# Seven products instead of eight in half of the first matmul, another seven-product form in the second, and the second attention visit moved into the second matmul

## The chip, the cores and the metric

The kernel runs on one core of one Trainium2 chip. TensorE (PE in the profile) multiplies matrices out of SBUF into PSUM, VectorE (DVE) and ScalarE (ACT) read PSUM and do the elementwise work, GpSimd (POOL) scales the values and issues the loads, SyncE (SP) issues the stores and the transposing DMAs. The metric is the device time of one execution in microseconds (us), lower is better.

## The reference

Inputs are q, k, v of shape (batch 4, heads 8, sequence 768, head dimension 64), one decay per head, and two weight matrices, 512 x 2048 and 2048 x 512. A causal linear attention with decay is followed by a feed-forward block with exact GELU:

```
for each block of 64 positions:
    out   = ((q k^T) * Dmask) v  +  (q * lam^(pos+1)) state
    state = lam^64 * state + (k * lam^(63-pos))^T v
x = out, 3072 tokens x 512
y = gelu(x @ w_in) @ w_out
```

## The kernel before

The 3072 tokens are cut into 24 chunks of 128 positions; a group is four chunks, one of each batch entry, 512 tokens. There are six groups (`NG = 6`), and for each the two matmuls run as a list of blocks that `mlp_blocks(g)` returns. Attention for the groups to come is put between these blocks as "visits": short runs of small TensorE products on quarters of the array. A visit answers one pair of chunks (`answer_states`, `answer_values`), asks the next (`ask`: scores into the two `sc` banks) and makes the products of keys and values for the states (`ask_products`). The order is written by hand: `at(when, run)` gives each step a place in the sequence of blocks, measured in the work of the blocks, and the final loop issues each block after the steps that are due. Every engine executes what it is given in that order.

PSUM has eight banks of 128 x 512 f32, handed out by tag: two each of `sc`, `mh` and `mo`, one each of `o` and `t`. SBUF tiles rotate in the same way through their `bufs`.

For groups 1 to 5 before the change:

- First matmul (`mm1`, line 518): 16 blocks of 128 rows of w_in against 512 tokens. Eight of them (in group 1: twelve) run in pairs on halves of 256 tokens, low half first, since the high half of `x_t` arrives by the group's first visit; the rest run on 512 columns. Each result, one bank, goes through one GELU on ScalarE (line 521) into `g_t`.
- Second matmul (`blocks_by_seven`, products on line 414): 2 x 2 x 2 quarters of the product, by seven products of 16 matmuls each instead of eight. Five sums of quarters of `g_t` (`g_sum`, line 389) and five of w_out (`w_out_sum`, line 368, once) are made on VectorE, and the seven results are combined by two ScalarE copies and seven VectorE additions. Each product is emitted in two steps `u` = 0, 1 of eight matmuls (128 tokens each). In the last group the products `m1` and `m7` of the two `u` are held in two different banks (`banks["r"]`).
- Visits: the first of a group stands one block into it, the second eight or ten blocks into it, inside the first matmul. Group 1, which ends the attention start-up, has visits at 0, 4, 14 and 20 blocks.

Of the kernel before, what the change touches and what calls it, by code (L numbers as in the profile page):

```python
# [10 lines left out]
ALU = mybir.AluOpType  # L11
# [4 lines left out]
def kernel(  # L16
# [34 lines left out]
    g_pool = ctx.enter_context(tc.tile_pool(name="g", bufs=2))  # L51
# [37 lines left out]
    w_out_t = w_pool.tile([128, NK2, d_model], BF16)  # L89
    NS = 4  # L90
# [66 lines left out]
    def decay_v(c, eng):  # L157

        c.v_dec = work_pool.tile([128, H, D], BF16, tag="vd", name="v_dec", bufs=4)
        eng.tensor_mul(c.v_dec, c.v, lam_m[:, :, None].to_broadcast((128, H, D)))  # L160
# [180 lines left out]
    def empty_outputs(c):  # L341
# [6 lines left out]
        else:  # L348
# [9 lines left out]
    W_SUMS = {1: (B11, B22, ALU.add), 3: (B12, B22, ALU.subtract), 4: (B21, B11, ALU.subtract),  # L358
              6: (B11, B12, ALU.add), 7: (B21, B22, ALU.add)}

    def w_out_sum(i, half):

        if i not in wsum:
            wsum[i] = w_pool.tile([128, KH, DH], BF16, name=f"w_sum{i}")
        (ka, da), (kb, db), op = W_SUMS[i]
        n = KH // 2
        at = lambda ks: slice(ks.start + half * n, ks.start + (half + 1) * n)
        nc.vector.tensor_tensor(wsum[i][:, half * n:(half + 1) * n, :], w_out_t[:, at(ka), da], w_out_t[:, at(kb), db],
                                op=op)

    def w_out_sums():
        for i, half in [(6, 0), (6, 1), (7, 0), (1, 0), (3, 0), (4, 0), (7, 1), (1, 1), (3, 1), (4, 1)]:
            w_out_sum(i, half)

    def blocks_by_seven(g, g_t, first):
# [5 lines left out]
        G_SUMS = {6: (0, hi, 0, lo, ALU.subtract), 1: (0, lo, KH, hi, ALU.add), 2: (0, hi, KH, hi, ALU.add),  # L381
                  5: (0, lo, KH, lo, ALU.add), 7: (KH, lo, KH, hi, ALU.subtract)}

        def g_sum(i, k):
            if i not in gsum:
                gsum[i] = sum_pool.tile([128, KH, TH], BF16, tag=f"g{i}", name=f"g_sum{i}")
            ka, ta, kb, tb, op = G_SUMS[i]
            ks = slice(k, k + n4)
            nc.vector.tensor_tensor(gsum[i][:, ks, :], g_t[:, ka + k:ka + k + n4, ta], g_t[:, kb + k:kb + k + n4, tb],  # L389
                                    op=op)  # L390
# [3 lines left out]
        def with_sums(i, run):  # L394
            def both():
                run()
                if i in sums_at:
                    g_sum((5, 2, 1, 6, 7)[sums_at.index(i)], 0)
            return both

        sums_at = range(10, 15)
        blocks = [(with_sums(i, run), cost) for i, (run, cost) in enumerate(first)]

        left = {1: lambda k, t: gsum[1][:, k, t], 2: lambda k, t: gsum[2][:, k, t],
                3: lambda k, t: g_t[:, k, t], 4: lambda k, t: g_t[:, KH + k, TH + t.start:TH + t.stop],
                5: lambda k, t: gsum[5][:, k, t], 6: lambda k, t: gsum[6][:, k, t], 7: lambda k, t: gsum[7][:, k, t]}
        right = {2: lambda k: w_out_t[:, k, d_lo], 5: lambda k: w_out_t[:, KH + k, d_hi]}
        right.update({i: (lambda k, i=i: wsum[i][:, k, :]) for i in W_SUMS})
# [3 lines left out]
        def product(i, u, o, begin):  # L412
            for k in range(KH):
                nc.tensor.matmul(o, left[i](k, slice(u * C, (u + 1) * C)), right[i](k),  # L414
                                 start=(begin and k == 0), stop=(k == KH - 1), skip_group_check=True)

        def tile_f(name):
            sb[name] = sum_pool.tile([128, 2, DH], F32, tag=f"f_{name}", name=f"f_{name}")
            return sb[name]

        def store(rows, us, cols):
            b = slice(rows * 2 + us.start, rows * 2 + us.stop)
            dst = out_r[g, :, b, cols]
            nc.sync.dma_start(dst, sb["o0" if rows == 0 else "o1"][:, us, cols])
# [3 lines left out]
        def m3(u):  # L428
            if u == 0:
                banks["p"] = bank([128, 2, DH], F32, "mo", "p_ps")  # L430
            product(3, u, banks["p"][:, u, :], u == 0)
            if u == 1:
                nc.scalar.copy(tile_f("e"), banks["p"])
                g_sum(5, n4)

        def m4(u):
            if u == 0:
                banks["q"] = bank([128, 2, DH], F32, "mo", "q_ps")
            product(4, u, banks["q"][:, u, :], u == 0)
            if u == 0:  # L440
                g_sum(2, n4)
            else:
                nc.scalar.copy(tile_f("f"), banks["q"])

        def m5(u):
            if u == 0:
                banks["p5"] = bank([128, 2, DH], F32, "mo", "p5_ps")
                g_sum(1, n4)
            product(5, u, banks["p5"][:, u, :], u == 0)
            if u == 1:  # L450
                sb["o0"] = out_pool.tile([128, 2, d_model], F32, tag="o0", name="o0_sb", bufs=1)
                nc.vector.tensor_add(sb["o0"][:, :, d_hi], sb["e"], banks["p5"])  # L452
                nc.vector.tensor_sub(tile_f("x1"), sb["f"], banks["p5"])
                if last:
                    store(0, both, d_hi)

        def m2(u):
            if u == 0:
                banks["q2"] = bank([128, 2, DH], F32, "mo", "q2_ps")
            product(2, u, banks["q2"][:, u, :], u == 0)  # L460
            if u == 0:
                g_sum(6, n4)
            else:
                sb["o1"] = out_pool.tile([128, 2, d_model], F32, tag="o1", name="o1_sb", bufs=1)
                nc.vector.tensor_add(sb["o1"][:, :, d_lo], sb["f"], banks["q2"])
                nc.vector.tensor_sub(tile_f("x2"), sb["e"], banks["q2"])

        def m1(u):
            if u == 0:
                banks["s"] = bank([128, 2, DH], F32, "mh", "s_ps")  # L470
                if last:
                    banks["r"] = [bank([128, DH], F32, tag, "r_ps") for tag in ("mh", "t")]
                else:
                    r_ps = bank([128, 2, DH], F32, "mh", "r_ps")
                    banks["r"] = [r_ps[:, 0, :], r_ps[:, 1, :]]
                    banks["r_all"] = r_ps
            product(1, u, banks["r"][u], u == 0 or last)
            if u == 0:
                g_sum(7, n4)
            elif last:  # L480
                for w in range(2):
                    nc.vector.tensor_add(sb["x2"][:, w, :], sb["x2"][:, w, :], banks["r"][w])
            else:
                nc.vector.tensor_add(sb["x2"], sb["x2"], banks["r_all"])

        def m6(u):
            product(6, u, banks["s"][:, u, :], u == 0)
            if u == 1:
                nc.vector.tensor_add(sb["o1"][:, :, d_hi], sb["x2"], banks["s"])
                store(1, both, every)  # L490

        def m7(u):
            product(7, u, banks["r"][u], False)
            if last:
                nc.vector.tensor_add(sb["o0"][:, u, d_lo], sb["x1"][:, u, :], banks["r"][u])
# [370 lines left out]
```

## Time and profile before

| | |
|---|---|
| median of three runs | 202.98 us (200.58 to 205.71) |
| the profiled execution's own time | 201.34 us |
| span in the profile | 199.6 us, granted TensorE clock 0.999 |
| TensorE busy | 191.0 us, 96% of the span |
| VectorE busy | 120.4 us, 60% |
| ScalarE busy | 82.7 us, 41% |
| GpSimd busy | 110.5 us, 55% |
| group 0 and start-up | 0 to 50.4 us |
| groups 1, 2, 3, 4, 5 begin at | 50.4, 81.1, 110.3, 139.9, 168.9 us |

The page names one execution. A group's duration is read from the start of its first w_in product to that of the next. A row of matmuls in the timeline gives a start, the duration to the modelled end of the last one, and the count; the distance between starts of rows gives the pace.

### The profile page before, as it was taken

Reading aid. Unit: us, or ns where it says so; the run is one execution under the profiler, and the core shown is the slowest. Engines: PE = TensorE matmul, PEld = TensorE weight load, DVE = VectorE, ACT = ScalarE, POOL = GpSimd, SP = SyncE. Lnnn points to the kernel's source line nnn. Section 1 sums busy time; section 2 is a strip of 40 time slices with the busy share of each in tenths; the row PEclk is TensorE's granted clock in tenths of the full one; section 3 lists DMA queues with packets and bytes.
Section 4 is the critical chain, followed back from the end, with each engine's and each line's share of the span. In section 5 each row is a group of like instructions: output and inputs, shape, how many; then the busy total and the mean of one; then the engine's idle time right before and its main releaser. Section 6 shows DMA issues by size and latency. Waiting matters only on the chain.

```text
span 199.6 us, 5998 instructions
## 1 busy us (share of the span) xinstructions
PE 191.0 (96%) x2625; PEld 142.9 (72%) x2636; DVE 120.4 (60%) x206; ACT 82.7 (41%) x149; POOL 110.5 (55%) x136
## 2 busy tenths in 40 slices
PE   7699999999999999999999989999999999999992
PEld 2388674455887788885688875688884788865881
DVE  3753507764473869694949658649638358341482
ACT  4964564234556413174520255520355410566200
POOL 8999973499969799993493497591400000000000
PEclk9999999999999999999999999999999999999999
DMA  5999999999999999999799799899700002300014
GB/s 115 148 174 175 200 204 206 153 216 150 130 220 149 151 142 136 118 209 233 72 84 153 234 68 127 90 110 122 234 8 3 3 0 80 134 0 3 0 53 158
DMA packets 102761, 24.76 MB, mean 124 GB/s; under 512 B 93264, under 2 KB 99920, under 8 KB 102736
## 3 DMA queue, kind: packets, MB, share of 16 engines
q0 software_dynamic: 81072, 13.38, 99.3%
q1 hardware_dynamic: 21664, 11.02, 26.6%
q8 instruction: 20, 0.33, 0.7%
q14 instruction: 5, 0.04, 0.1%
HBM read 27.27 MB, written 6.29 MB: 168 GB/s over the span
## 4 chain that ended last, share of the span: by engine, by line
PE 73%; DMA 10%; POOL 10%; DVE 4%; issue 1%; POOLq 0%; DVEq 0%
PE h_ps L518 35%; PE r_ps L414 8%; PE p_ps L414 8%; PE q_ps L414 8%; DMA q_t<-in_q_dram 6%; DMA w_out_t<-in_moe_w_out_dram 4%; PE s_ps L414 4%; POOL w_in_t L94 3%; PE o_ps L531 3%; POOL k_t L70 2%; POOL q_t L70 2%; POOL v_t L70 2%; PE o_ps L314 2%; POOL v_dec L160 1%; PE kv_ps L290 1%
## 5 line engine op out<-in xcount | busy, mean ns | idle before, releaser
L518 PE MATMUL h_ps<-x_t,w_in_t 128*128 128x256 bf16 (+3 forms) x648 | 87.5, 290 | 1.0 <-issue 0.6
L521 ACT ACTIVATE g_t<-h_ps 128x512 bf16<-128x512 f32 (+2 forms) x99 | 57.8, 584 | 72.6 <-PE h_ps L518 72.6
L518 PEld LDWEIGHTS <-w_in_t 128*128 128x128 bf16 x656 | 58.4, 98 | 23.8 <-issue 1.0
L389 DVE TENSOR_TENSOR g_sum<-g_t 128x1024 bf16<-128x1024 bf16 x50 | 33.4, 713 | 16.4 <-ACT g_t L521 16.4
L414 PEld LDWEIGHTS <-g_sum 128*128 128x128 bf16 x400 | 39.1, 98 | 4.8 <-issue 0.3
L160 POOL TENSOR_TENSOR v_dec<-v_t,lam_m 128x512 bf16<-128x512 bf16 x23 | 24.3, 1094 | 25.6 <-PE o_ps L326 14.8
L70 POOL DMA_DIRECT2D v_t<-in_v_dram x24 | 22.2, 927 | 3.1 <-DMA w_out_t<-in_moe_w_out_dram 1.7
L414 PE MATMUL r_ps<-w_sum,g_sum 128*128 128x256 bf16 x160 | 19.1, 273 | 0.1
L73 POOL DMA_DIRECT2D k_t<-in_k_dram x24 | 18.7, 799 | 0.0
L73 POOL DMA_DIRECT2D q_t<-in_q_dram x24 | 18.3, 788 | 0.0
L414 PEld LDWEIGHTS <-g_t 128*128 128x128 bf16 x160 | 15.6, 98 | 2.9
L531 PE MATMUL o_ps<-w_out_t,g_t 128*128 128x512 bf16 x61 | 14.5, 379 | 0.4 <-issue 0.3
L333 DVE TENSOR_TENSOR x_t<-o_ps,lam_q 128x512 bf16<-128x512 f32 x16 | 10.6, 683 | 3.9 <-PE o_ps L314 3.9
L70 POOL DMA_DIRECT2D k_t<-in_k_dram x12 | 11.2, 933 | 1.9 <-DMA w_out_t<-in_moe_w_out_dram 1.6
L70 POOL DMA_DIRECT2D q_t<-in_q_dram x12 | 10.9, 908 | 2.4 <-DMA w_out_t<-in_moe_w_out_dram 2.4
L531 PEld LDWEIGHTS <-g_t 128*128 128x128 bf16 x64 | 5.9, 98 | 6.3
L305 DVE TENSOR_TENSOR sc_m<-sc_ps,cmask_d 128x512 bf16<-128x512 f32 x16 | 10.3, 679 | 0.0
L452 DVE TENSOR_TENSOR o_sb<-f_e,p_ps 128x512 f32<-128x512 f32 x5 | 3.4, 686 | 11.0 <-issue 11.0
L582 PE MATMUL idle_ps<-idle 128*128 128x256 bf16 (+1 forms) x40 | 8.7, 353 | 1.2 <-DVE idle L107 1.2
L414 PE MATMUL p_ps<-w_out_t,g_sum 128*128 128x256 bf16 x80 | 9.6, 273 | 0.0
L414 PE MATMUL s_ps<-w_sum,g_sum 128*128 128x256 bf16 x80 | 9.6, 273 | 0.0
L414 PE MATMUL q_ps<-w_out_t,g_sum 128*128 128x256 bf16 x80 | 9.6, 273 | 0.0
(90 smaller groups left out, 192.2 us busy)
## 6 DMA issues: line engine op xcount, KB each, us to landing
out_dram<-o_sb SPq DMA_DIRECT2D x9, 512.0 KB, 4.9
v_t<-in_v_dram POOLq DMA_DIRECT2D x24, 128.0 KB, 5.6
w_out_t<-in_moe_w_out_dram POOLq DMA_DIRECT2D x4, 512.0 KB, 10.3
w_in_t<-in_moe_w_in_dram POOLq DMA_DIRECT2D x7, 256.0 KB, 7.3
k_t<-in_k_dram POOLq DMA_DIRECT2D x12, 128.0 KB, 6.5
q_t<-in_q_dram POOLq DMA_DIRECT2D x12, 128.0 KB, 6.8
k_t<-in_k_dram POOLq DMA_DIRECT2D x24, 64.0 KB, 4.8
q_t<-in_q_dram POOLq DMA_DIRECT2D x24, 64.0 KB, 5.0
```

Of the source, the lines that this page charges most:

```text
L70: nc.gpsimd.dma_start(raw[n, name], chunk_of(name, n))
L73: nc.gpsimd.dma_start(raw[n, name][:, r::2, :], chunk_of(name, n)[:, r * HP:(r + 1) * HP, :])
L94: nc.gpsimd.dma_start(w_in_t[:, :, f], w_in_r[:, :, f])
L160: eng.tensor_mul(c.v_dec, c.v, lam_m[:, :, None].to_broadcast((128, H, D)))
L305: nc.vector.tensor_mul(w.sc_m[:, hi], w.sc_ps[hi], cmask_d[:, None, None, :].to_broadcast((128, 2, HP, D)))
L333: nc.vector.tensor_mul(x[:, :, :, HALVES[t]], pairs[n].o_ps[t], lam_q[:, :, None, HALVES[t]].to_broadcast((128, HP, 2, D)))
L389: nc.vector.tensor_tensor(gsum[i][:, ks, :], g_t[:, ka + k:ka + k + n4, ta], g_t[:, kb + k:kb + k + n4, tb], op=op)
L414: nc.tensor.matmul(o, left[i](k, slice(u * C, (u + 1) * C)), right[i](k), start=(begin and k == 0), stop=(k == KH - 1), skip_group_check=True)
L518: nc.tensor.matmul(h_ps[:, k, :], w_in_t[:, ki, (kf + k) * 128:(kf + k + 1) * 128], x_t[:, ki, cols], start=(k == 0 and ki == 0), stop=(ki ...
L521: nc.scalar.activation(g_t[:, kf:kf + ks, cols], h_ps, ACT.Gelu)
L531: nc.tensor.matmul(om[io], g_t[:, kf, io * C:(io + 1) * C], w_out_t[:, kf, :], start=(kf == 0), stop=(kf == NK2 - 1))
L582: nc.tensor.matmul(idle_ps[0][:, :cols], idle[:, :128], idle[:, :cols], start=True, stop=True)
```

## The change

1. The second half of the first matmul of groups 1 to 5 (row blocks 4 to 7 and 12 to 15) is done by seven products too. `w_in_sums` makes four sums of w_in once; `x_sums` makes four sums of quarters of `x_t` in each group. Two `Step`s of seven products of four matmuls each work in three PSUM banks (`ha`, `hb`, `hc`): a product is written to a bank, copied to SBUF by ScalarE (`kept`), and the next product is accumulated onto the same bank. VectorE adds (`total`), and GELU reads three of the four results from SBUF. The other half of the first matmul stays plain, in pairs on 256 tokens, with the high-half blocks in the banks `t` and `o`.
2. The second matmul's seven products take a form with four sums of `g_t` and four of w_out. Three of its results are again accumulated onto a bank that has been read. The last two products, `m7` and `m4`, are read in two steps: after each `u` of `m7` VectorE adds that half of the bank, after each `u` of `m4` ScalarE copies it.
3. `g_t` becomes one tile, not two in rotation; `v_dec` has six buffers, not four.
4. The second visits stand 20 or 22 blocks into the group (21 in group 1), inside the second matmul, and the steps around them move: masks, sums of states, emptied outputs, GpSimd's `decay_v`. In group 1 the key-value products of the visit at 4 blocks take the `sc` banks.
5. In group 1 the products 7 and 4 of the second matmul are issued in halves of 128 columns.

The diff, cut to its core:

```diff
-    W_SUMS = {1: (B11, B22, ALU.add), 3: (B12, B22, ALU.subtract), 4: (B21, B11, ALU.subtract),
-              6: (B11, B12, ALU.add), 7: (B21, B22, ALU.add)}
+    W_SUMS = {1: (B12, B11), 2: (B22, 1), 3: (B22, B12), 4: (B21, 2)}
...
+    def first_blocks(g, g_t, x_t, mm1):
...
+        def x_sums():
+            for i in (1, 2, 3, 4):
+                x_s[i] = sum_pool.tile([128, 2, TH], BF16, tag=f"x{i}", name=f"x_sum{i}")
...
+                nc.vector.tensor_sub(x_s[i], a, b)
...
+            def product(self, i, b, tag=None):
+                if tag:
+                    self.banks[b] = bank([128, 2, TH], F32, tag, f"{b}_ps")
+                for k in range(2):
+                    for q in range(2):
+                        nc.tensor.matmul(self.banks[b][:, k, :], left[i](q, self.kf + k), right[i](q),
+                                         start=(tag is not None and k == 0 and q == 0), stop=(q == 1),
+                                         skip_group_check=True)
...
+            def kept(self, name, b):
+                self.sb[name] = sum_pool.tile([128, 2, TH], F32, tag=f"f_{name}", name=f"h_{name}", bufs=2)
+                nc.scalar.copy(self.sb[name], self.banks[b])
+            def total(self, name, b):
+                nc.vector.tensor_add(self.sb[name], self.sb[name], self.banks[b])
...
+            def p1(self):
+                self.product(1, "ha", "mh")
+                self.kept("p1", "ha")
+            def p2(self):
+                self.product(2, "hb", "mo")
+                self.total("p1", "hb")
+            def p5(self):
+                self.product(5, "hc", "mo")
+                self.kept("p5", "hc")
+            def p6(self):
+                self.product(6, "ha")
+                self.kept("u2", "ha")
+            def p3(self):
+                self.product(3, "hc")
+                self.total("u2", "hc")
+                self.gelu(0, lo, self.sb["p1"])
+            def p7(self):
+                self.product(7, "ha")
+                self.total("p5", "ha")
+                self.gelu(0, hi, self.sb["u2"])
+            def p4(self):
+                self.product(4, "ha")
+                self.gelu(KH, hi, self.sb["p5"])
+                self.gelu(KH, lo, self.banks["ha"])
+        x, y = Step(KW[0]), Step(KW[2])
...
+        plan = [(run, plain) for run in los]
+        plan += [(then_sums(x.p1) if g == 1 else x.p1, plain // 2), (his[0], plain)]
+        plan += [(x.p2, plain // 2), (x.p5, plain // 2), (his[1], plain)]
+        plan += [(run, plain // 2) for run in (x.p6, x.p3, y.p1, x.p7, y.p2, y.p5, x.p4, y.p6, y.p3)]
+        plan += [(his[2], plain), (y.p7, plain // 2), (his[3], plain), (y.p4, plain // 2)]
...
         def product(i, u, o, begin):
+            parts = [slice(0, DH // 2), slice(DH // 2, DH)] if g == 1 and i in (4, 7) else [slice(0, DH)]
...
+        def m6(u):
+            g_sum(3, u * n4)
+            chain(6, "a", u)
+            if u == 1:
+                nc.scalar.copy(tile_f("u2"), banks["a"])
+        def m3(u):
+            chain(3, "c", u)
+            if u == 1:
+                nc.vector.tensor_add(sb[0][:, :, d_hi], sb["u2"], banks["c"])
+                store(0, both, every)
+        def m7(u):
+            chain(7, "a", u)
+            nc.vector.tensor_add(sb[1][:, u, d_hi], sb["p5"][:, u, :], banks["a"][:, u, :])
+            if last and u == 1:
+                store(1, both, d_hi)
+        def m4(u):
+            chain(4, "a", u)
+            nc.scalar.copy(sb[1][:, u, d_lo], banks["a"][:, u, :])
+            if last:
+                store(1, slice(u, u + 1), d_lo)
+            elif u == 1:
+                store(1, both, every)
-        blocks += [((lambda f=f, u=u: f(u)), KH * DH) for f in (m3, m4, m5, m2, m1, m6, m7) for u in range(2)]
+        blocks += [((lambda f=f, u=u: f(u)), KH * DH) for f in (m1, m2, m5, m6, m3, m7, m4) for u in range(2)]
...
-        e: [reorder_powers, triangles, w_out_sums, lambda: decay_v(live[4], nc.vector)],
+        e: [reorder_powers, triangles, w_out_sums, w_in_sums, lambda: decay_v(live[4], nc.vector)],
...
-             (new_states, M, M + 2), states_of=(M, M + 2), kv_tags="mo mo")
+             (new_states, M, M + 2), states_of=(M, M + 2), kv_tags="sc sc")
...
-        w = g + (10 if g == 2 else 8) * B
+        w = g + (22 if g == NG - 2 else 20) * B
-        steps((w, pair_visit, done, asked), (w, mid_states, asked))
+        steps((w, pair_visit, done, asked, "mh mh", nc.scalar.copy), (g + 22 * B, mid_states, asked))
```

More of the change, by code (lines that the diff above doesn't have):

```diff
@@ L89 @@
     w_out_t = w_pool.tile([128, NK2, d_model], BF16)
+    g_t = w_pool.tile([128, NK2, M * C], BF16)
     NS = 4
@@ L392, in blocks_by_seven @@
+            nc.vector.tensor_tensor(gsum[i][:, ks, :], part(a), part(b), op=op)
         n4 = KH // 2
[L394 to L406, printed above, removed]
@@ L432, in m3, with m2 @@
             if u == 1:
-                nc.scalar.copy(tile_f("e"), banks["p"])
-                g_sum(5, n4)
-        def m4(u):
+                nc.scalar.copy(tile_f("p1"), banks["a"])
+        def m2(u):
             if u == 0:
[L438 to L443, printed above, removed]
+                banks["b"] = bank([128, 2, DH], F32, "mh", "b_ps")
+            chain(2, "b", u, True)
+            if u == 1:
+                for r in range(2):
+                    sb[r] = out_pool.tile([128, 2, d_model], F32, tag=f"o{r}", name=f"o{r}_sb", bufs=1)
+                nc.vector.tensor_add(sb[0][:, :, d_lo], sb["p1"], banks["b"])
@@ L457, in m2 @@
[L457 to L484, printed above, removed]
```

180 lines of the change are left out of this document (110 added, 70 removed).

## The prediction

> **What bounds the kernel now.** I read the page's busy shares first, then its chain, then the timeline where the change cuts in. All times are in us.
>
> ```profile
> span 199.6 us, 5998 instructions
> PE 191.0 (96%) x2625; PEld 142.9 (72%) x2636; DVE 120.4 (60%) x206; ACT 82.7 (41%) x149; POOL 110.5 (55%) x136
> PE 73%; DMA 10%; POOL 10%; DVE 4%; issue 1%; POOLq 0%; DVEq 0%
> ```
>
> TensorE is busy 96% of the span and holds 73% of the chain; the DMA and GpSimd shares lie in the start-up before 50. From 50.4 to 195.8 it runs almost without a gap, so a matmul saved there is time saved, and any wait put into TensorE's order is time lost in full. Group 4 and the end of group 5 show the pace and the handovers:
>
> ```profile
> 142.01 6.29 PE L518 MATMUL h_ps<-x_t,w_in_t 128*128 128x256 bf16 x56
> 142.19 1.29 DVE L333 TENSOR_TENSOR x_t<-o_ps,lam_q 128x512 bf16<-128x512 f32 x2 [0.80 <-PE o_ps L314]
> 143.10 0.60 ACT L521 ACTIVATE g_t<-h_ps 128x512 bf16<-128x512 f32 x1 [1.54 <-PE h_ps L518]
> ...
> 149.40 7.08 PE L518 MATMUL h_ps<-x_t,w_in_t 128*128 128x512 bf16 x31
> ...
> 156.32 1.91 PE L414 MATMUL p_ps<-w_sum,g_t 128*128 128x256 bf16 x16
> 158.06 1.91 PE L414 MATMUL q_ps<-w_sum,g_t 128*128 128x256 bf16 x16
> ...
> 193.88 1.91 PE L414 MATMUL r_ps<-w_sum,g_sum 128*128 128x256 bf16 x16
> ...
> 194.96 0.42 DVE L495 TENSOR_TENSOR o_sb<-f_x,r_ps 128x256 f32<-128x256 f32 x1 [0.18 <-PE r_ps L414]
> 195.83 0.42 DVE L495 TENSOR_TENSOR o_sb<-f_x,r_ps 128x256 f32<-128x256 f32 x1 [0.45 <-PE r_ps L414]
> ```
>
> A 256-column matmul takes (158.06 - 156.32)/16 = 0.109 and a 512-column one (156.32 - 149.40)/32 = 0.216 (one of 32 records is missing). The first eight of r_ps end at 193.88 + 0.875 = 194.755 and their reader starts at 194.96: 0.205 from TensorE to VectorE (the same for ScalarE: 142.01 + 0.875, then 143.10). The other direction shows once, where TensorE waits to accumulate onto a bank that VectorE still reads:
>
> ```profile
> 78.57 0.68 DVE L484 TENSOR_TENSOR f_x<-f_x,r_ps 128x512 f32<-128x512 f32 x1
> ...
> 79.30 1.91 PE L414 MATMUL r_ps<-w_sum,g_sum 128*128 128x256 bf16 x16
> ```
>
> The read ends at 79.25, the next product starts 0.05 later. This is the one place where the old second matmul waits for a reader, and it costs about 0.25. Last, spacing and ScalarE's sizes: two VectorE operations of 0.68 take 1.29, so 0.60 each in a row, and two ScalarE copies of 0.586 take 1.07 (at 47.42), so 0.49 each. Half a bank on ScalarE costs 0.38:
>
> ```profile
> L521 ACT ACTIVATE g_t<-h_ps 128x256 bf16<-128x256 f32 x4 | 1.5, 384 | 1.5 <-PE h_ps L518 1.5
> ```
>
> **The change, part by part.** *Matmuls saved.* Before, the first matmul of groups 2 to 5 is 64 matmuls of 256 columns and 32 of 512: 7.00 + 6.92 = 13.92. After it is 64 + 56 of 256: 13.13, so -0.79 each. Group 1 (96 and 16) goes from 13.96 to 13.13, -0.83. The second matmul keeps its 112 products. Sum **-4.0**, sure to 0.1. The 128-column halves in group 1 are 64 matmuls for 32: by the 128-column h_ps row (112 in 7.4) at most +0.7, by half a 256-column one nothing; I take +0.15.
>
> *Three waits at the end of every group.* `m7` and `m4` accumulate onto bank `a`, and the halves u = 0 and 1 lie in that one bank. In the changed kernel's instruction list the first matmul of m7(1) waits for VectorE's addition of m7(0), the first of m4(0) for the addition of m7(1), the first of m4(1) for ScalarE's copy of m4(0). Nothing else stands in TensorE's order between them, so it is idle each time. VectorE: 0.205 + 0.42 + 0.05 = 0.675, twice; ScalarE: 0.205 + 0.38 + 0.05 = 0.635. Together 1.99 a group, **+9.95** for five. Queued behind is all of TensorE: the rest of the group, and the next group's first block, its GELU and visit. Bounds: at least the three readings alone, 1.22 x 5 = 6.1; at most one other operation of 0.60 ahead of the reader once a group, 13. The old form's wait at 79.30 goes: -0.25.
>
> The Trainium skill bears on this ("PSUM — Partial Sum Buffer", section "PSUM bank collisions raise a hardware error"): a read and a matmul's write must be kept apart by bank and quadrant, not by address, so halves of columns in one bank do not count as apart. The row at 79.30 agrees as far as it goes, but there the reader took the whole bank; no row here shows a half. By that rule the three waits are needed and the sum is the one below; guarded by address they would fall away, the rival under (b).
>
> *In-place chains in the first matmul.* In a `Step`, p7 must wait for the copy of p6 out of `ha`: 0.205 + 0.59 + 0.05 = 0.85 if ScalarE is free, with p3 and y.p1 (0.875) between in x, y.p3 and his2 (1.31) in y. p4 must wait for VectorE's `total`: 0.205 + 0.69 + 0.05 = 0.95, with 0.875 between in both. So x.p4 and y.p4 lose 0.07 each bare. The cover is thin: ScalarE has 22 operations of 0.49 in this stretch, 10.8 beside TensorE's 13.1, and 15 of them stand in a row from his1 on. Following its queue from there (his1's GELU 0.2 after that block's end, then u2 copy, GELU, y.p1 copy, GELU, y.p5 copy, two GELUs, y.u2 copy), the x copy is 0.04 late and the y copy 0.1, and `new_states` ahead of y's totals on VectorE adds up to 0.15 in group 2. That is 0.25 to 0.45 a group, I take 0.35, **+1.75**; bounds 0 and, with ScalarE at 0.60 instead of 0.49 each, 1.0 a group. GELU from SBUF in f32 has no row; the nearest, exp from SBUF, is 0.62 against 0.597, inside this.
>
> *x_sums in group 1.* There they stand behind the visit's whole tail on VectorE:
>
> ```profile
> 55.67 8.39 PEld L518 LDWEIGHTS <-w_in_t 128*128 128x128 bf16 x72
> 55.78 0.69 DVE L345 CAST x_t<-o_ps 128x512 bf16<-128x512 f32 x1 [2.81 <-PE o_ps L255]
> ...
> 56.39 1.28 DVE L234 TENSOR_TENSOR tmp<-kv_ps,state 128x512 f32<-128x512 f32 x2
> ...
> 57.59 1.57 DVE L240 TENSOR_TENSOR state<-tmp,lam_c 128x512 bf16<-128x512 f32 x2
> ```
>
> The visit ends at 55.67. x.p1 runs to 56.11; his0 now needs x_t's high half at once, 55.78 + 0.69 + 0.05 = 56.52: +0.41. Then his0 and x.p2 run to 57.83, and x.p5 needs x_sum1, which starts when the states are done, 59.08. 128 x 512 bf16 has no row: between half and all of g_sum's 0.71, I take 0.45, so 59.58: +1.75. Sum **+2.15**, bounds 1.4 and 2.5. In groups 2 to 5 x_sum1 is ready about 1 before x.p5 (visit end, then two x_t and two state operations of 0.60), so there it costs nothing.
>
> *Nothing, with its cover.* w_in_sums adds 4 x 0.60 to VectorE and two fewer w_out sums take off 1.2, at a place where it then sat idle for 1.25 until the values came:
>
> ```profile
> 39.68 0.69 DVE L160 TENSOR_TENSOR v_dec<-v_t,lam_m 128x512 bf16<-128x512 bf16 x1 [1.25 <-DMA v_t<-in_v_dram]
> ```
>
> Without that cover it is at most 1.2. The moved visit takes 1.25 of TensorE (148.13 to 149.40) wherever it stands; past the second matmul's sums it finds its banks emptied, and VectorE needs some 13 of operations in about 15 there, tight but ahead of TensorE. GpSimd gives out as many loads and `decay_v` as before, ahead of their use by more than half a group; SyncE as many DMAs. In the last group 256 KB more are stored within the last 3, but behind 512 KB which then go out earlier: 0, at worst 0.5.
>
> Sum: -4.0 + 0.15 + 9.95 - 0.25 + 1.75 + 2.15 = **+9.75**. The profiled execution's span of 199.6 becomes 209.4, its 201.34 becomes 211.1. It lay 0.8% under the median shown, 202.98, which would become 212.7. I give **212.0**, between the two.
>
> **Rivals.** (a) ScalarE sets the first matmul too. If its operations with waits don't overlap, 22 x 0.60 = 13.2 equals TensorE's 13.1, and each group loses 1.0 instead of 0.35, with VectorE's readers at their upper bound in part: +9.75 + 3.25 + 1 = 14, 216. For: 15 operations in a row, each with a semaphore. Against: the ScalarE rows in a row here do overlap. (b) The other side, not slower: the three waits cost nothing, because the halves of a bank can be read and written side by side and TensorE passes. m4(0) would then need only m7(0)'s addition, done 0.2 before m7(1) ends. It decides from the point where a wait is under 0.1: 9.75 - 9.95 = -0.2, 202.5. Against: the waits in the instruction list. With the first matmul's chains at their lower bound as well, -2, 200.7. (c) The waits bite, but less, at their lower bound, and group 1's too: 9.75 - 3.85 - 0.75 - 1.0 = +4.1, 206.5. For: handovers that I read off are from modelled matmul ends.
>
> **How the numbers follow.** Forecast 0.75; (a) 0.11; (b) 0.05; (c) 0.09. The forecast's own range is +8 to +11.5 on a base of 201.3 to 203: 209.3 to 214.5. To hold 8 in 10 I reach into (a) and part of (c): **207.5 to 216**. 2%, 4.1, is about what a measurement of this kernel can tell from no change. Slower by over 2%: forecast, (a) and most of (c), 0.93. Within 2%: most of (b) and the rest of (c), 0.06. Faster by over 2% needs all of the 4.0 and more: 0.01.
>
> **What would show it.** Right: in each of groups 1 to 5, the rows of a_ps broken into four runs of eight with gaps of about 0.65 to 0.7, released by VectorE, VectorE, ScalarE; TensorE's busy time down by some 4 and its idle time up by some 13; x_sum1 in group 1 released late, with a gap of about 1.7 before hc_ps; small gaps of 0.05 to 0.25 before ha_ps. Groups 2 to 5 are about 1.5 longer each, group 1 about 3.7. Wrong: a_ps in runs of 16 without gaps; gaps of a microsecond and more before ha_ps (then ScalarE or VectorE bounds the first matmul); a wait on loads or kT, qT at the moved visits.

## The result and the profile after

The changed kernel takes 212.05 us, median of four runs (211.29 to 212.57), against 202.62 of the kernel before (200.58 to 205.71). The ratio is 1.0497, with a 95% interval of 1.0407 to 1.0588: slower by 5%. The forecast was 212.0. All times below are in us. Medians are of all executions; the ratios leave out the executions that took over 1.5% longer than the fastest of the same kernel.

The page of the changed kernel, with the lines that answer to those of before (span, busy time and count of each engine, shares of the chain):

```profile
span 210.0 us, 6395 instructions
PE 193.1 (92%) x2768; PEld 153.8 (73%) x2772; DVE 130.7 (62%) x228; ACT 101.7 (48%) x197; POOL 111.9 (53%) x136
PE 61%; DVE 15%; POOL 11%; DMA 7%; issue 3%; ACT 1%; DVEq 0%; POOLq 0%
```

TensorE fell from 96% busy to 92%, and VectorE's share of the chain rose from 4% to 15%: TensorE now waits for it. How long and where is said by the view of waits of TensorE from 50 on (who waits, for whom, us in total, times, longest):

```profile
PE a_ps L526 <- DVE o_sb L584: 5.5, 10, 0.9
PE a_ps L526 <- ACT o_sb L590: 2.3, 5, 0.5
PE hc_ps L424 <- DVE x_sum L401: 1.2, 1, 1.2
...
PE ha_ps L424 <- DVE h_p L433: 0.2, 1, 0.2
```

Ten waits for the addition of m7, five for the copy of m4, one for x_sum. These figures count from the end of the matmul before as the profile models it, and that end lies some 0.16 too late (a row of eight is given 1.04, and rows that follow each other start 0.875 apart); from start to start of the rows the loss is seen whole. The end of group 2 in the timeline, TensorE first (the last row is group 3's first block), then its readers:

```profile
111.71 1.04 PE L526 MATMUL a_ps<-w_sum,g_sum 128*128 128x256 bf16 x8
113.26 1.03 PE L526 MATMUL a_ps<-w_sum,g_sum 128*128 128x256 bf16 x8 [0.51 <-DVE o_sb L584]
114.81 1.03 PE L526 MATMUL a_ps<-w_sum,g_t 128*128 128x256 bf16 x8 [0.51 <-DVE o_sb L584]
116.30 1.03 PE L526 MATMUL a_ps<-w_sum,g_t 128*128 128x256 bf16 x8 [0.46 <-ACT o_sb L590]
117.17 1.04 PE L611 MATMUL h_ps<-x_t,w_in_t 128*128 128x256 bf16 x8
...
112.79 0.42 DVE L584 TENSOR_TENSOR o_sb<-f_p,a_ps 128x256 f32<-128x256 f32 x1
114.33 0.42 DVE L584 TENSOR_TENSOR o_sb<-f_p,a_ps 128x256 f32<-128x256 f32 x1 [1.12 <-PE a_ps L526]
...
115.88 0.37 ACT L590 COPY o_sb<-a_ps 128x256 f32<-128x256 f32 x1 [5.12 <-PE a_ps L526]
```

Eight matmuls need 0.875, but the rows start 1.55, 1.55 and 1.49 apart: 0.675, 0.675 and 0.62 lost. The addition of 112.79 to 113.21 lies between the end of one row and the start of the next at 113.26, and so on: matmul, reader, matmul, one after the other.

What each group took, from its first w_in product to that of the next:

| | before | after | difference |
|---|---|---|---|
| up to group 1 | 50.38 | 51.66 | +1.28 |
| group 1 | 30.72 | 34.10 | +3.38 |
| group 2 | 29.21 | 31.41 | +2.20 |
| group 3 | 29.58 | 30.42 | +0.84 |
| group 4 | 29.00 | 30.64 | +1.64 |
| group 5, to TensorE's end | 26.91 | 28.36 | +1.45 |
| TensorE's end to the end of the span | 3.78 | 3.44 | -0.34 |

### The profile page after: what moved, and what is told of

Its sections match the earlier page's. It is cut to its first block, busy times and chain, and to the rows that moved or that the text cites. A ratio compares the mean times of both kernels' runs of the same rounds, so it can differ in the third digit from the quotient of the medians.

```text
span 210.0 us, 6395 instructions
## 1 busy us (share of the span) xinstructions
PE 193.1 (92%) x2768; PEld 153.8 (73%) x2772; DVE 130.7 (62%) x228; ACT 101.7 (48%) x197; POOL 111.9 (53%) x136
## 4 chain that ended last, share of the span: by engine, by line
PE 61%; DVE 15%; POOL 11%; DMA 7%; issue 3%; ACT 1%; DVEq 0%; POOLq 0%
PE a_ps L526 16%; PE h_ps L611 14%; PE ha_ps L424 7%; PE c_ps L526 7%; DMA w_out_t<-in_moe_w_out_dram 7%; PE b_ps L526 4%; PE hc_ps L424 3%; POOL w_in_t L94 2%; PE o_ps L624 2%; DVE o_sb L584 2%; POOL v_dec L160 2%; POOL k_t L69 2%; POOL q_t L69 2%; POOL v_t L69 2%; DVE g_sum L507 2%
## 5 line engine op out<-in xcount | busy, mean ns | idle before, releaser
L611 PE MATMUL h_ps<-x_t,w_in_t 128*128 128x256 bf16 (+3 forms) x479 | 55.5, 265 | 0.3 <-DVE x_t L345 0.2
L614 ACT ACTIVATE g_t<-h_ps 128x512 bf16<-128x512 f32 (+2 forms) x59 | 34.0, 576 | 24.4 <-PE h_ps L611 24.3
L526 PEld LDWEIGHTS <-g_sum 128*128 128x128 bf16 x336 | 31.3, 98 | 7.2 <-issue 3.8
L526 PE MATMUL a_ps<-w_sum,g_sum 128*128 128x256 bf16 (+1 forms) x176 | 20.1, 263 | 2.9 <-DVE o_sb L584 2.9
L424 PEld LDWEIGHTS <-wi_sum 128*128 128x128 bf16 x160 | 15.6, 97 | 4.3 <-issue 1.8
L507 DVE TENSOR_TENSOR g_sum<-g_t 128x1024 bf16<-128x1024 bf16 x20 | 14.3, 742 | 3.8 <-ACT g_t L614 3.8
L526 PE MATMUL a_ps<-w_sum,g_t 128*128 128x256 bf16 (+1 forms) x96 | 10.4, 254 | 4.9 <-DVE o_sb L584 2.6
L436 ACT ACTIVATE g_t<-h_p 128x512 bf16<-128x512 f32 x20 | 12.7, 636 | 0.5 <-DVE h_p L433 0.5
L333 DVE TENSOR_TENSOR x_t<-o_ps,lam_q 128x512 bf16<-128x512 f32 x16 | 10.4, 684 | 4.2 <-PE o_ps L314 4.2
L433 DVE TENSOR_TENSOR h_u<-h_u,hc_ps 128x512 f32<-128x512 f32 x10 | 6.9, 686 | 8.8 <-ACT h_u L430 8.7
L424 PE MATMUL ha_ps<-x_sum,wi_sum 128*128 128x256 bf16 x80 | 12.0, 272 | 0.0
```

Of the source, the lines that this page charges most:

```text
L333: nc.vector.tensor_mul(x[:, :, :, HALVES[t]], pairs[n].o_ps[t], lam_q[:, :, None, HALVES[t]].to_broadcast((128, HP, 2, D)))
L424: nc.tensor.matmul(self.banks[b][:, k, :], left[i](q, self.kf + k), right[i](q), start=(tag is not None and k == 0 and q == 0), stop=(q == 1),
L433: nc.vector.tensor_add(self.sb[name], self.sb[name], self.banks[b])
L436: nc.scalar.activation(g_t[:, k0 + self.kf:k0 + self.kf + 2, cols], src, ACT.Gelu)
L507: nc.vector.tensor_tensor(gsum[i][:, ks, :], part(a), part(b), op=op)
L526: nc.tensor.matmul(o[:, d], left[i](k, slice(u * C, (u + 1) * C)), right[i](k)[:, d], start=(begin and k == 0), stop=(k == KH - 1), skip_g ...
```

## The experiments

The theory: in this program TensorE does not accumulate onto a bank before the engine that reads it is done, and m7 and m4 give it nothing else to do in that time. The rivals: the loss belongs to the switch between halves or the small reads themselves; VectorE is simply too busy; the seven products of the first matmul are what costs.

### Two banks in the last group

```diff
-                banks["a"] = bank([128, 2, DH], F32, "mo", "a_ps")
+                if last:
+                    banks["a2"] = [bank([128, DH], F32, tag, "a_ps") for tag in ("mo", "t")]
+                else:
+                    banks["a"] = bank([128, 2, DH], F32, "mo", "a_ps")
...
-            nc.vector.tensor_add(sb[1][:, u, d_hi], sb["p5"][:, u, :], banks["a"][:, u, :])
+            nc.vector.tensor_add(sb[1][:, u, d_hi], sb["p5"][:, u, :], a_half(u))
...
-            nc.scalar.copy(sb[1][:, u, d_lo], banks["a"][:, u, :])
+            nc.scalar.copy(sb[1][:, u, d_lo], a_half(u))
```

> Changed kernel, but in the last group alone the two token halves of m1, m6, m7 and m4 lie in two PSUM banks; every half is still read by itself, at the same place in the order. Theory (TensorE may not accumulate onto a bank while another engine reads that bank): in group 5 the three gaps of 0.68, 0.68 and 0.62 before a_ps vanish, since m7(0)'s addition and m4's first copy then lie beside the other half's eight matmuls (0.875 each); groups 1 to 4 keep theirs. Span about 210.0 - 2.0 = 208.0. Rival (the loss belongs to the switch between the halves, or to the small reads themselves, wherever they lie): nothing changes, 210.

The last group's second matmul went from 14.36 to 12.39, by 1.97, exactly the three gaps. (In this profile the granted clock was 0.83 on the mean from 60 to 70, in group 1, so the last group is compared and not the span of 210.9.) The timeline of its end, TensorE's rows and then VectorE's:

```profile
202.08 1.91 PE L526 MATMUL c_ps<-w_out_t,g_sum 128*128 128x256 bf16 x16
203.82 1.91 PE L526 MATMUL a_ps<-w_sum,g_sum 128*128 128x256 bf16 x16
205.57 1.91 PE L526 MATMUL a_ps<-w_sum,g_t 128*128 128x256 bf16 x16
...
204.90 0.42 DVE L598 TENSOR_TENSOR o_sb<-f_p,a_ps 128x256 f32<-128x256 f32 x1
205.77 0.42 DVE L598 TENSOR_TENSOR o_sb<-f_p,a_ps 128x256 f32<-128x256 f32 x1 [0.45 <-PE a_ps L526]
```

The rows of a_ps are whole, and the readers of 0.42 are still there, beside the matmuls of the other half. What costs is that both halves lie in one bank, not the reads and not the switch between halves. The two banks are also two tiles of the program, and two tiles in one bank were not run, so bank and tile are not told apart here. Whether the chip would need the wait for two halves of one bank was not tried either: the waits stand in the program, and a kernel without them could have a race.

### Whole reads, and m3 in between

```diff
-            nc.vector.tensor_add(sb[1][:, u, d_hi], sb["p5"][:, u, :], banks["a"][:, u, :])
+            if last:
+                nc.vector.tensor_add(sb[1][:, u, d_hi], sb["p5"][:, u, :], banks["a"][:, u, :])
+            elif u == 1:
+                nc.vector.tensor_add(sb[1][:, :, d_hi], sb["p5"], banks["a"])
...
             elif u == 1:
+                nc.scalar.copy(sb[1][:, :, d_lo], banks["a"])
```

> Changed kernel, but in groups 1 to 4 m7 is read by one addition of the whole bank after both halves, and m4 by one copy after both. Theory: one wait per group in place of three, between m7(1) and m4(0), of 0.205 + 0.69 + 0.05 = 0.945; so groups 2 to 4 are 1.03 shorter each, group 1 about 1.4: span about 205.5. Rival (the switch between halves costs): the gaps before m7(1) and m4(1) stay, and the span is 210 or a little over.

As foretold, one wait is left in each of groups 1 to 4. In the timeline of group 2's end (TensorE, then its reader):

```profile
112.50 1.91 PE L526 MATMUL a_ps<-w_sum,g_sum 128*128 128x256 bf16 x16
115.19 1.91 PE L526 MATMUL a_ps<-w_sum,g_t 128*128 128x256 bf16 x16 [0.78 <-DVE o_sb L587]
...
114.45 0.69 DVE L587 TENSOR_TENSOR o_sb<-f_p,a_ps 128x512 f32<-128x512 f32 x1 [0.99 <-PE a_ps L526]
```

115.19 - 112.50 - 1.75 = 0.94, against 0.945. The second matmul of groups 2 to 4 is shorter by 1.03 each (15.58, 15.57 and 15.86 become 14.55, 14.55 and 14.83). Group 1's is shorter by 0.45 only, not by some 1.4: ahead of the reader on VectorE stood `state`, with both inputs in SBUF, which took 1.53 in place of 0.69 beside two products of GpSimd. The span is 207.9, not 205.5. Group 2's first matmul grew from 15.84 to 18.24, a new wait, told below; that and group 1's missing 0.95 are partly hidden by a start of group 1 that came 1.2 earlier in this execution, where the two kernels do not differ.

```diff
-        blocks += [((lambda f=f, u=u: f(u)), KH * DH) for f in (m1, m2, m5, m6, m3, m7, m4) for u in range(2)]
+        blocks += [((lambda f=f, u=u: f(u)), KH * DH) for f, u in (
+            (m1, 0), (m1, 1), (m2, 0), (m2, 1), (m5, 0), (m5, 1), (m6, 0), (m6, 1), (m3, 0), (m7, 0), (m7, 1), (m3, 1),
+            (m4, 0), (m4, 1))]
```

> As the one before, and in all groups the order is m6(0), m6(1), m3(0), m7(0), m7(1), m3(1), m4(0), m4(1): the halves of m3, 0.875 each and in another bank, stand where m7 and m4 would wait for their reader. Theory: the remaining wait of 0.945 shrinks to 0.07 in groups 1 to 4, m7(0)'s wait for the copy of m6 (0.845) stays covered; in group 5, which still reads by halves, one of three waits (0.68) is covered too. 210.0 - 8.0 - 0.7 = 201.3 of span, with up to 1 more at the very end, because the store of 512 KB of the last group is issued 1.75 later. Rival (the time went to VectorE's load, not to the order): under half of this, 206 or more.

205.77 against 202.01 of before, ratio 1.0191 (1.0131 to 1.0252), span 204.1 against an expected 201.3. The waits ahead of a_ps are 0.12 to 0.14 a group in groups 1 to 4, and 1.36 in the last. The engines do the same work, and only the size of the reads and the order differ, yet the second matmuls are shorter by 8.2 in sum (77.75 to 69.51): VectorE's load was not the cause. But group 2's first matmul now takes 19.05, which takes 3.2 of it back.

### GpSimd's products beside VectorE's

The rows in group 2 of the kernel just shown, VectorE and then GpSimd:

```profile
88.10 0.69 DVE L301 TENSOR_TENSOR tmp<-kv_ps,mid 128x512 f32<-128x512 f32 x1
88.71 3.70 DVE L401 TENSOR_TENSOR x_sum<-x_t 128x512 bf16<-128x512 bf16 x1
92.45 0.42 DVE L401 TENSOR_TENSOR x_sum<-x_t,x_sum 128x512 bf16<-128x512 bf16 x1
...
88.95 3.17 POOL L160 TENSOR_TENSOR v_dec<-v_t,lam_m 128x512 bf16<-128x512 bf16 x3
```

`x_sum` has both inputs in SBUF. One takes 3.70 and the next, of the same size, 0.42. The long one covers GpSimd's three products. In the changed kernel two x_sums of 1.14 and 1.15 lie beside three such products in the same way.

```diff
+        if g == 2:
+            at(v, lambda n=n: [decay_v(live[m], nc.vector) for m in (n + 2, n + 3)])
...
-        steps((g + 7 * B, decays, n + 2, n + 3))
+        if g > 2:
+            steps((g + 7 * B, decays, n + 2, n + 3))
...
-            steps((g + 7 * B, decayed, n + M, n + M + 1), (g + 8 * B, prefetch, n + M + 3),
+            steps((g + 7 * B, begun, n + M, n + M + 1), (g + (8.5 if g == 2 else 7) * B, decays, n + M, n + M + 1),
+                  (g + 8 * B, prefetch, n + M + 3),
```

> The kernel with whole reads and m3 in between, but in group 2 the v_dec of chunks 14 and 15 are made by VectorE right after the first visit, and those of 16 and 17 by GpSimd only after the loads of chunks 18 and 19 are issued. In the runs so far x_sum (0.42 alone) took 1.14 and 1.15 in one and 3.70 in another where it lay beside GpSimd's v_dec (3.25 and 3.17 for three), while VectorE's operations that read PSUM kept 0.68. Theory: an operation of VectorE with both inputs in SBUF in bf16 waits while GpSimd's elementwise product runs; without it there x_sum is 0.42 to 0.45 again, the first matmul of group 2 goes from 19.05 to 15.7 to 16, the span from 204.1 to about 201. Rival (x_sum waits for its data, the high half of x_t, and the profile books this as its duration): x_sum stays at over 1 and group 2 at 19.

204.08 in the median, ratio 1.0106 (1.0040 to 1.0171), span 203.1 where about 201 was expected. The same place on VectorE:

```profile
89.25 0.69 DVE L301 TENSOR_TENSOR tmp<-kv_ps,mid 128x512 f32<-128x512 f32 x1
89.86 0.41 DVE L401 TENSOR_TENSOR x_sum<-x_t 128x512 bf16<-128x512 bf16 x1
```

x_sum is 0.41 again, with the same operations ahead of it in both kernels and x_t written as long before: it did not wait for its data. The first matmul of group 2 took 16.74, not 15.7 to 16: 1.6 of gaps stand at its visit. The second took 14.59 in place of 13.80, since two products of GpSimd (2.73 at 102.00) now lie beside two sums of g_t, which take 2.98 where two take 1.28 alone. The cause of the long x_sum is shown; the gain is partly given back at the next place.

The Trainium skill says this on its page "SBUF — State Buffer", section "Who interferes with whom": a VectorE instruction with two inputs in SBUF contends with a GpSimd instruction that reads SBUF, and one with at most one such input does not (outside modes that use both ports). The rows above agree (3.70 beside 3.17, 0.41 without), and so does VectorE's tmp, which reads one input from PSUM and keeps its 0.69.

### The old second form with the new first matmul

```diff
-        blocks += [((lambda f=f, u=u: f(u)), KH * DH) for f in (m1, m2, m5, m6, m3, m7, m4) for u in range(2)]
+        blocks += [((lambda f=f, u=u: f(u)), KH * DH) for f in (m3, m4, m5, m2, m1, m6, m7) for u in range(2)]
...
+                if i == len(first) - 1:
+                    g_sum(5, 0)
+                    g_sum(2, 0)
```

> Changed kernel with the second matmul in its old form (seven products, five sums of g_t, each result in its own bank, the order of before); the first matmul by seven products and the second visits inside the second matmul stay. The sums of g_t are moved to the end of the first matmul and into the first products of the second. Theory: the three waits (10.3 with group 1's longer first one) go, and nothing else: what stays of the rest is -4.0 for the matmuls, +1.8 in group 1 (x_sums, and the high half of x_t), +1.8 before ha_ps, +0.85 in group 0, +0.43 at the start. Span about 199.8, the same as before's 199.6. It is up to 2 longer if the sums of g_t, which now all come after the first matmul's last blocks, are late on VectorE (gaps ahead of p5_ps, q2_ps or r_ps). Rival (the seven products of the first matmul are what costs the time): 205 and more.

211.73 in the median, ratio 1.0440 (1.0367 to 1.0514). The expectation of 199.8 of span was wrong by about ten: the executions had 208.1 to 212.4. (The one with the profile had 211.8; its granted clock was 0.60 from 60 to 64, in group 1's first matmul, and 0.63 from 118 to 121.3, at the end of group 2, so these two places are left out.) The total lies where the rival put it, at 205 and more, but not for the rival's reason. The first matmul, the same code in both kernels, stayed near the changed kernel's times (15.85, 15.12, 14.79 and 13.94 in groups 2 to 5, after 15.84, 14.84, 14.78 and 14.00), so what is lost against the expectation is not lost there. What the seven products themselves are worth is not told by this run: in group 5, where no visit moved, the first matmul takes 14.00 with them and took 14.52 without, and for group 1 the last run below answers. The last group's second matmul, with no visit in it, took 12.39, as before. The loss is in the second matmul of the other groups (16.08 in group 3, where the kernel before takes 12.23 and has no visit of some 1.4 in it), and the view of waits of TensorE from 100 on names two causes (this run, then the next one); 2.2 of the wait for f_x stands in group 2, behind a g_sum of 2.27 beside GpSimd's v_dec:

```profile
PE r_ps L526 <- DVE f_x L601: 3.2, 3, 2.2
PE r_ps L526 <- DVE mid L296: 3.0, 2, 1.5
```

```diff
-    w = g + (22 if g == NG - 2 else 20) * B
+    w = g + 17 * B
```

> The kernel with the old second form, but from group 2 on the second visit stands in the middle of m4, three steps earlier. In the old-second run TensorE waited 1.66 ahead of r_ps in groups 2 and 3, until VectorE had emptied the visit's kv_ps out of the two banks that s_ps and r_ps take. Theory: this wait goes, 1.7 less in each of groups 2 and 3; the second wait ahead of r_ps (2.39 in group 2, a g_sum of 2.27 beside GpSimd's v_dec) is another cause and may stay or move. Rival (r_ps waits for its sum of g_t in both cases): no gain.

```profile
PE r_ps L526 <- DVE f_x L601: 2.9, 3, 1.0
PE o_ps L314 <- issue: 1.1, 2, 0.9
```

208.36, ratio 1.0330 (1.0282 to 1.0378), span 206.2. The wait for mid is gone: it was the two banks, which the moved visit fills and VectorE empties late. The wait for f_x, the addition of the whole of r_ps that the old form had at 79.30, stayed, at up to 1.0 a time where it had been 0.25: it now stands behind other work on VectorE. So the old form does not fit around a visit either. Which of the two second forms is better there is not settled by a kernel with hand-moved sums.

### Group 1 and group 0

```diff
+            plan += [(then_sums(x.p1), plain // 2), (x.p2, plain // 2), (his[0], plain)]
...
-        e: [reorder_powers, triangles, w_out_sums, w_in_sums, lambda: decay_v(live[4], nc.vector)],
+        e: [reorder_powers, triangles, w_out_sums, lambda: decay_v(live[4], nc.vector)],
...
-        e + 14: [lambda: visit([4, 5], []), lambda: empties(4, 5)],
+        e + 14: [lambda: visit([4, 5], []), lambda: empties(4, 5), w_in_sums],
...
-    visit_at(1 + 4 * B, [2 * M - 2, 2 * M - 1], [], (empties, 2 * M - 2, 2 * M - 1), (sums, M, M + 2),
-             (new_states, M, M + 2), states_of=(M, M + 2), kv_tags="sc sc")
+    visit_at(1 + 4 * B, [2 * M - 2, 2 * M - 1], [], (empties, 2 * M - 2, 2 * M - 1),
+             states_of=(M, M + 2), kv_tags="sc sc")
+    steps((1 + 4.25 * B, sums, M, M + 2), (1 + 4.25 * B, new_states, M, M + 2))
```

> Changed kernel with two rows of sums moved. In group 1 the x_sums are issued to VectorE ahead of tmp and state (which now follow x.p1), and x.p2, which needs only the low half of x_t, stands before his0. In group 0 w_in_sums are issued after the visit at e + 14, not before the values of chunk 4. Theory: in group 1 the gaps of 1.41 before hc_ps and 0.41 before h_ps go: -1.8. In group 0 qT is no longer late: the 0.85 by which the second matmul of group 0 grew goes, if the four sums fit into VectorE's idle 2.66 at 47.7. Together span 210.0 - 2.6 = 207.4. Rival (the states are needed as soon as the sums, so the wait only changes its place): group 1 stays at 34.1.

212.58, ratio 1.0571 (1.0522 to 1.0619), span 210.4: no gain at all. In group 1 the gaps of 1.41 and 0.41 went, as expected, but y's hb_ps now waited 1.56 for x's total, which stood on VectorE behind tmp and state. In group 0 the four wi_sums took 1.15, 0.69, 1.58 and 1.52, two of the long ones beside a v_dec of GpSimd, not 0.60 each (the one of 1.58, at 48.06, begins before the next v_dec, at 49.35, and has no such cause on record), and TensorE waited 1.7 for qT behind them. The rival was right: the wait changed its place.

```diff
-    parts = [slice(0, DH // 2), slice(DH // 2, DH)] if g == 1 and i in (4, 7) else [slice(0, DH)]
+    parts = [slice(0, DH)]
```

> Changed kernel, with products 7 and 4 of group 1 on 256 columns as in the other groups. Forecast: 64 matmuls of 128 columns become 32 of 256, between 0 and 0.7 less (0.15 was taken), and the first gap before a_ps in group 1, 1.05 where the other groups have 0.68, falls to 0.68: group 1's second matmul goes from 16.38 to 15.6 to 15.9. Rival (the longer gap comes from a late sum of g_t on VectorE): the gap stays at 1.05.

Group 1's second matmul took 16.36 against 16.38, and the first gap stayed at 1.07 (the granted clock was 0.91 on the mean from 120 to 140 of this profile, in group 3, so its span of 215.0 is not compared). The halves of 128 columns cost nothing. The longer gap is VectorE's queue, though not a sum of g_t: in the changed kernel's timeline x_t stands ahead of the reader:

```profile
80.73 0.68 DVE L333 TENSOR_TENSOR x_t<-o_ps,lam_q 128x512 bf16<-128x512 f32 x1
81.33 0.41 DVE L584 TENSOR_TENSOR o_sb<-f_p,a_ps 128x256 f32<-128x256 f32 x1
```

### All of it together

Four kernels joined the parts: whole reads with m3 between in groups 1 to 4, two banks in the last group, sums and v_dec moved.

> All of it in one kernel: whole reads with m3 in between in groups 1 to 4, two banks in the last group with its old order, the earlier sums of group 1 and the later ones of group 0, and group 2's v_dec elsewhere. Sum on the kernel with m3 in between (204.1): -1.8 in group 1, -0.85 in group 0, -3.2 in group 2, -1.36 in group 5: span 196.9, time 198.6, against 202.0 of before, so 1.7% faster. Rival (each removed wait uncovers another, on VectorE): 200 or more of span.

203.15, ratio 1.0090 (1.0058 to 1.0122), span 202.5 where 196.9 was expected. The last group came to 12.39. New waits stood in group 0 (1.0 for qT, behind a wi_sum of 2.00), group 1 (1.1 ahead of hb_ps, and 1.7 inside a_ps with no releaser) and group 2 (0.85 ahead of kv_ps, behind a g_sum beside v_dec).

> All mended, once more, with what that run showed: x.p1's total issued to VectorE ahead of tmp and state in group 1 (hb_ps waited 1.12 for it), the third sum of w_in moved to group 1's start (qT was 1.0 late behind a wi_sum of 2.00), 256 columns throughout (a gap of 1.73 inside a_ps of group 1), and group 2's v_dec of chunks 16 and 17 on VectorE near the group's end (a g_sum took 3.2 beside GpSimd's, and kv_ps waited 0.85). Sum 202.5 - 1.1 - 1.0 - 1.7 - 0.85 = 197.9 of span, time 199.6, 1.1% under the time before. Rival (VectorE's queue is the bound there and each wait moves on): 200 to 202, no faster than before.

203.35, ratio 1.0078 (1.0038 to 1.0118), span 200.8. The four named waits went, and 1.8 ahead of hc_ps, 1.0 ahead of a_ps and 1.6 inside a visit came.

> All mended, a third time. In group 1 tmp is issued to VectorE after the first three totals and state after the fourth (a total waited behind them, and hc_ps 1.78 for it); in group 2 the v_dec of chunks 16 and 17 follow the masks (they took 2.45 beside GpSimd's own v_dec, and a_ps waited 1.04). Sum 200.8 - 1.78 - 0.92 = 198.1 of span, time 199.9; 196.7 and 198.5 if a stall of 1.4 in TensorE, for which the trace names no releaser and which each run has in another place, does not fall into it. The time before was 202.1: 1 to 1.8% faster. Rival (in a queue without room each wait moves on): 200.5 or more of span, no faster.

203.52 in the median, ratio 1.0042 (1.0000 to 1.0084), where 199.9 was expected. In all three runs the rival held by the medians: waits went where they were treated, and others came.

> The third mended kernel, but group 1 keeps the first matmul of the kernel before (16 blocks, none of the seven products), with tmp and state back behind the first visit; the sums of w_in, now needed from group 2 on, are made in group 1 at 7 blocks, where VectorE has nothing to do. Theory: in group 1, where the high half of x_t, the state sums and the seven products' own sums all come due on VectorE together, the seven products cost more than the 0.83 they save; group 1's first matmul goes from 17.7 to 17.9 back to 16.5 (as before), group 0's second from 18.4 to 18.8 to 18.3 (bar a stray stall of 1.0), the rest stays: PE's end at about 50.4 + 16.5 + 14.1 + 30.2 + 28.5 + 28.8 + 26.4 = 194.9, against 195.8 of before; span 198.3, time 200.1, 0.9% faster than 202.0. Rival (the stray stalls of 1.0 to 1.6 decide): 200 of span, the same as before.

202.71 in the median, ratio 1.0022 (0.9986 to 1.0058): the time before, as the rival had it, not the 0.9% less that was expected. Group 1's first matmul is back at 16.51, as the theory had it (17.72 in the changed kernel, 17.88 in the third joined one), and TensorE ends at 196.51, which holds a stall of 1.75 in group 2's first visit and 1.0 more than usual in group 0. None of the versions beats the kernel before.

## Why the prediction was right

*Three waits a group.* Forecast 1.99 a group, 9.95 in all. Measured 1.97 in groups 2 to 5 (0.675 + 0.675 + 0.62) and 2.34 in group 1, together 10.2. What the upper bound allowed for, another operation ahead of the reader, happened once, with x_t in group 1. That the halves' common bank makes the wait was shown by two banks, that the order leaves it uncovered by m3 in between. The rule of the Trainium skill that was weighed there ("PSUM — Partial Sum Buffer", section "PSUM bank collisions raise a hardware error") gave the sum that came out; the rival by address, with 202.5, fell. The runs show that the program waits, not that the chip would have to.

*Matmuls saved.* Forecast 0.79 a group. In group 5 the first matmul went from 14.52 to 14.00, while its gaps rose from 0.34 to 0.62: 0.52 + 0.28 = 0.80. The second matmul of that group without its waits, 14.36 - 1.97 = 12.39, is that of before to the hundredth.

*The old wait.* The 0.25 at 79.30 is gone, as forecast.

*In-place chains.* Forecast 0.35 a group, 1.75 in all. The gaps ahead of ha_ps were 0.27 in groups 3 to 5, 0.22 in group 1, and in group 2, with hc_ps, 0.99: 2.0. The sum was right, in part by luck: four groups were under the 0.35 and one at nearly three times it. Group 2's part was named (state operations ahead of y's totals on VectorE) but sized at 0.15 where some 0.45 shows: its gap ahead of ha_ps is 0.72 also in the kernel in which x_sum is short.

*x_sums in group 1.* Forecast 0.41 + 1.75. Measured 0.41 and 1.41. x.p5 was due where I had it (59.14, the group lying 1.28 later), but x_sum1 was ready 0.3 sooner: the two state operations took 1.28 where the row of before had 1.57.

*What I costed at nothing.* The moved visits met no wait, as forecast. The 128-column halves: 0.15 forecast, nothing measured. The w_in_sums did cost something in this execution. I let what they add, 2.4 less the 1.2 of two w_out sums, hide in an idle stretch of 1.25 behind the w_out sums. That took for granted that the w_out sums run in a row, as before. Here VectorE waited 1.56 for a load of w_out between them, so the idle time lay ahead of the sums and not behind them; they reached into the time of qT, and TensorE's scores waited for it (VectorE, then TensorE, in the changed kernel):

```profile
37.60 1.42 DVE L370 TENSOR_TENSOR w_sum<-w_out_t,w_sum 128x1024 bf16<-128x1024 bf16 x2 [1.56 <-DMA w_out_t<-in_moe_w_out_dram]
...
41.60 0.68 DVE L388 TENSOR_TENSOR wi_sum<-w_in_t 128x1024 bf16<-128x1024 bf16 x1
42.20 0.69 DVE L160 TENSOR_TENSOR v_dec<-v_t,lam_m 128x512 bf16<-128x512 bf16 x1
42.80 1.28 DVE L172 TENSOR_TENSOR qT<-t_ps,lam_q 128x512 bf16<-128x512 bf16 x2
...
43.54 0.42 PE L200 MATMUL sc_ps<-qT,kT 64*64 64x128 bf16 x16 [0.42 <-DVE qT L172]
```

Group 0's second matmul went from 18.59 to 19.44: +0.85, inside the 1.2 that I named for the case that the cover is gone. But most of it goes with the load, not with the sums. Seven more profiles have the w_in_sums at this place. Where VectorE waited 1.83 for loads of w_out in all (the kernel with full columns; 1.81 here) this matmul took 19.46, after a wait of 1.30 it took 18.96, and in the other five, with 0.54 at most, 18.23 to 18.86. So the experiment that moved these sums, and the 0.85 that the joined kernels were to gain, set out from a loss that comes and goes with the execution. Whether the new order of the w_out sums brings the wait is open: the old order shows none in three profiles. Another 0.43 lies in the start-up, where the change does nothing.

*The sum.* +9.75 was forecast for the span, 10.4 measured. On the way +0.85 and +0.43 that I had not, and -0.73 (a stall of TensorE at 115.24 in the execution before, which did not come again) and -0.34 at the end, nearly cancel. With the terms as measured, 9.8, that makes 10.0; the last 0.4 is spread over the groups, and no run names it. So the close agreement of 212.0 and 212.05 owes something to chance, as does group 3's +0.84 and group 2's +2.20 where some 1.5 was forecast for each; that of the terms of the second matmul does not.

*A sign that failed.* I expected TensorE's busy time to fall by 4 and its idle time to rise by 13. Busy time rose by 2.1. The page counts a row up to its modelled end, 1.04 for eight matmuls that follow each other at 0.875, so each of the fifteen rows that is broken off adds about 0.16 of busy time that is none, 2.4 in all; and of before 11 records of matmuls are missing (2625 beside 2636 weight loads). That doesn't add up to the whole of it, but it shows that starts of rows are the measure.

## What to carry to other kernels

When a result is accumulated onto a bank that is read in between, count from the end of the matmul through the reader to the next matmul (here 0.205 + 0.42 + 0.05) and put matmuls on another bank into that time; reading in smaller pieces makes it worse unless the pieces lie in different banks. Before sums are added to save matmuls, ask of the place where they come due whether the engine that makes them has the time there: seven products save 0.83 of matmuls in group 1, and with their sums its first matmul takes 1.2 longer than without them. Where several engines run near their limit in one stretch, a wait taken away is mostly found again at the next operation of the same queue, so each move is worth what the next wait leaves of it.

## What the runs showed of the hardware that I had not expected

An elementwise operation of VectorE with both inputs in SBUF stretched from 0.42 to 3.70 beside three of GpSimd, while those that read PSUM kept their 0.68; nothing in the view of waits of VectorE shows it, only the duration.

TensorE has stalls of 0.6 to 1.8 for which the trace names no releaser, one or two in most runs and in different places, most of them inside a visit. Eight of them were compared with the instruction queue: each ends 2.4 to 3.1 after a transfer on it of some 16 KB (for example, in the last run, a transfer at 82.6 and a stall from 83.76 to 85.51). Most such transfers are followed by no stall. That the stalls are late instructions is a guess; no run tested it. The Trainium skill ("Runtime: NRT & Kernel Launch", section "Instruction fetch mechanics") has instructions fetched in blocks of 16 KiB, mostly hidden; the size agrees, the rest is open.
